# Attention units in another order on TensorE: matmuls grouped by tile shape, one reduction on GpSimd

## The chip, the cores and the metric

The kernel runs on one core of one Trainium2 chip. The metric is device time in microseconds (us) of one execution, the median of several runs. TensorE (PE) multiplies into PSUM; VectorE (DVE), ScalarE (ACT) and GpSimd (POOL) do the rest; SyncE (SP) issues the DMAs that this document speaks of.

## The reference

```python
def _attn_ref(q, k, v):                      # batch 4, heads 8, seq 576, head_dim 64
    q_d, k_d, v_d = means over groups of 4 positions          # 144 positions
    out_d = sm_attn(q_d, k_d, v_d)                            # full softmax, pooled
    out_up = np.repeat(out_d, 4, axis=2)
    mask = np.abs(pos[:, None] - pos[None, :]) < 4
    out_local = softmax(where(mask, q k^T / 8, -1e9)) v       # 7 keys per query
    return out_up + out_local

def reference(**kwargs):
    x = _attn_ref(q, k, v)        # as 2304 rows of 512
    x = _moe_ref(x, ...)          # soft MoE, 8 experts, 4 slots each: x @ phi, two softmaxes
    return _moe2_ref(x, ...)      # top-2 MoE, 8 experts, 512 -> 1024 -> 512
```

## The kernel before, in words

The program has three stages: the attention (about 0 to 160 us of the span), the soft MoE (to about 200), the top-2 MoE (the rest). The change touches the first alone.

The attention works on 16 **units**, each one batch and two heads. The loop over `p` from -1 to 14 walks the string `SEQ` of step names; the table `BL` gives each name its function and its offset: step f with offset d works on unit p - d. The end, units 13 to 15, is written out in `TSEQ`. Each engine gets its instructions in this order and works them off in order; nothing reorders them. All line numbers are those of the kernel before.

The steps, by engine:

- `ld` (L186, SP): queries and keys of unit p+2, four DMAs in pieces of 256 bytes, into one of two buffers. `lV` (L207, SP): values of unit p+1, four DMAs, into one of two buffers, whose readers `VD` and `DP` of unit p-1 stand in the same p. `W` (L101, SP): one half of a matrix of the soft MoE, 1 MB, in two or four DMAs. SP's order is ld, W, lV in each p.
- `A0`, `A1` (L231, PE): keys and queries of unit p+1 turned (12 passes); `a0x`, `a1xx`: copies out of PSUM into K and Q. `DQ0`, `DQ1` (L249 and L251 on POOL, L245 on DVE): sums of four neighbouring queries of each head; `KD` (L257, L258, POOL): the same of the keys.
- `S` (L285, L289, PE): the mask, then the scores of unit p, 40 passes of 35 columns in tiles of 128x64. `M`, `EL`, `EX`, `SU`, `P0`, `P1`: softmax on DVE, ACT, DVE and POOL (L333).
- `SD` (L300, PE): pooled scores; `MD`, `DX`, `RD`, `DM`: their softmax (L339 DVE, L351 ACT, L358 DVE, L365 POOL).
- `CP`, `CD` (L375, L386, PE): the two probability matrices of unit p-1 turned; `EPxx`, `EDx`: copies out.
- `VD` (L268, L272, PE): pooled values, in tiles of 128x32; `V0`, `V1`: copies out. `DP` (L414, PE): local product, tiles of 64x64; `x0`, `x1`: copies out. `DD` (L421, PE): pooled product, two heads by two blocks of 128 and 16 keys; `XA` (L433, DVE): adds it.
- `EP` (L441, L443, PE): the finished unit p-2 turned; `LG` (L463, L465, PE): its part of x @ phi, four matmuls with 32 columns of phi and one with phi four times side by side; `LA` (L474, DVE): adds it up.
- `ST`, `SU_`, `SK` (L506, L519, L534): once per batch, the softmax over rows and its product.

The helper `cp` puts a copy on DVE when its name is in `ON_V`, else on ACT. PSUM has four buffers `t`, one `S`, one `Sd`, one `xl` of two banks.

Of the kernel before, what the change touches and what calls it, by code (L numbers as in the profile page):

```python
# [25 lines left out]
ON_V = ['a110', 'a111', 'p00', 'v0', 'v1']  # L26
# [11 lines left out]
def attn_moe_moe_kernel(ctx: ExitStack, tc: tile.TileContext, q, k, v, moe_phi, moe_w1, moe_w2,  # L38
# [10 lines left out]
    NG = 10  # L49
# [40 lines left out]
    phi4 = const.tile([128, 4, 4 * NS], F32, name="phi4")  # L90
# [24 lines left out]
    with ExitStack() as tctx:  # L115
# [34 lines left out]
        P = a2.tile([128, NG, 64], F32, name="P")  # L150
        Vs = [(a1, a2)[i].tile([128, 5, 2, D], F32, name=f"V{i}") for i in range(2)]
# [27 lines left out]
        LD, VQ, KD, DQ, SD, SS, PD, PL, XL, XT, XK = ({} for _ in range(11))  # L179
# [81 lines left out]
        def v_pe(u):  # L261
# [21 lines left out]
        def b_s(u):  # L283
            s = ps.tile([128, 512], F32, name="S")
            nc.tensor.matmul(s[:, 0:NG * KW], idb, mask.rearrange("p g k -> p (g k)"), start=True, stop=True)  # L285
# [6 lines left out]
            SS[u] = s  # L292
# [87 lines left out]
        def c_d(u):  # L380
# [8 lines left out]
            PdT = wk.tile([128, 2, 2, 144], F32, name="PdT", bufs=1)  # L389
            CT[u, 1] = (PdT, tt)  # L390
# [8 lines left out]
        def c_ed(u, kb):  # L399
            PdT, tt = CT[u, 1]  # L400
# [36 lines left out]
        def e_pe(u):  # L437
# [148 lines left out]
        for p in range(-1, NU - 1):  # L586
# [8 lines left out]
            for nm in SEQ:  # L595
# [8 lines left out]
                if p == -1 and nm == "lV":  # L604
                    nc.gpsimd.memset(PT, 0.0)
# [797 lines left out]
```

## Time and profile before

| what | us |
|---|---|
| median of three runs (lowest, highest) | 496.54 (495.12, 497.39) |
| the profiled execution | 494.55 |
| its span, first to last instruction | 492.7 |
| attention: first score matmul (S of unit 0) to the soft MoE's first product (L795) | 8.42 to 164.37 |
| PE busy, share of the span | 470.2, 95% |
| DVE, ACT, POOL busy | 277.4, 263.4, 199.2 |

A time in a row is counted from the span's start. Matmuls overlap, so the time that a step takes on PE is read from its start to the start of the next step, not from its own duration.

### The profile page before, as it was taken

To read this page: it belongs to the slowest core of one execution; us is meant where nothing else is said; L and a number is where in the kernel's file an instruction comes from. 1 tells how busy PE (TensorE), PEld (TensorE's weight loads), DVE (VectorE), ACT (ScalarE), POOL (GpSimd) and SP (SyncE) were. 2 spreads that over 40 slices of the span, in tenths; PEclk is the share of its full clock that TensorE was granted. 3 is DMA by queue.
4 is the path that set the end of the run, shared out by engine and by line. 5 is a ranking of instruction groups with operands and counts; after the bars stand their busy time and mean duration, and the time that the engine had idled before them with its cause. 6 is when DMAs were issued, how large, how long until landed. Compare 5 with 4: busy or idle time off the path is not lost.

```text
span 492.7 us, 12033 instructions
## 1 busy us (share of the span) xinstructions
PE 470.2 (95%) x4569; PEld 355.9 (72%) x4569; DVE 277.4 (56%) x720; ACT 263.4 (53%) x698; POOL 199.2 (40%) x289
## 2 busy tenths in 40 slices
PE   5999999899998999899999999999999999999993
PEld 4688877777875543467787787887887887878882
DVE  7878877777875321696579545273462544624300
ACT  2567766666775021486365465483664746727410
POOL 5565636536540100166566677422222221222222
PEclk9999999999999799999999999999999999999997
DMA  9999998989979599999988744699958856333333
GB/s 160 278 243 214 233 221 192 242 216 202 265 239 345 171 393 399 389 346 338 365 258 228 224 75 76 150 363 297 275 72 229 216 128 154 43 45 43 45 43 46
DMA packets 108423, 104.16 MB, mean 211 GB/s; under 512 B 68170, under 2 KB 78090, under 8 KB 108362
## 3 DMA queue, kind: packets, MB, share of 16 engines
q1 hardware_dynamic: 101450, 90.50, 61.2%
q0 software_dynamic: 6912, 12.85, 16.6%
q8 instruction: 38, 0.62, 0.5%
q14 instruction: 23, 0.19, 0.1%
HBM read 83.60 MB, written 19.73 MB: 210 GB/s over the span
## 4 chain that ended last, share of the span: by engine, by line
PE 73%; issue 9%; DMA 7%; DVE 3%; POOL 2%; ACT 2%; POOLq 2%; SPq 0%; ACTq 0%; DVEq 0%
PE y L1054 34%; DMA wr<-in_moe_w_dram 5%; PE S L289 4%; PE t L231 3%; PE gx L871 3%; PE xl L421 3%; PE Sd L300 3%; PE xl L414 2%; PE t L375 2%; PE xl L268 2%; PE t L441 2%; PE h L1034 2%; PE t L386 2%; POOL out_dram L1073 2%; POOLq L1079 1%
## 5 line engine op out<-in xcount | busy, mean ns | idle before, releaser
L1054 PE MATMUL y<-whi,hl 128*128 128x512 f32 x320 | 127.3, 398 | 0.0
L1054 PE MATMUL y<-whi,hh 128*128 128x512 f32 x320 | 126.7, 396 | 0.4 <-ACT hh L1035 0.4
L1054 PE MATMUL y<-wlo,hh 128*128 128x512 f32 x320 | 126.5, 395 | 0.0
L1073 POOL DMA_INDIRECT out_dram<-ys,idx x40 | 64.5, 1612 | 107.9 <-ACT ys L1065 56.3
L1065 ACT ACTIVATE ys<-y,gt 128x512 f32<-128x512 f32 x40 | 27.4, 686 | 82.4 <-issue 46.9
L1026 DVE TENSOR_TENSOR wlo<-wr,whi 128x512 fp32r<-128x512 f32 x64 | 42.0, 692 | 50.3 <-ACT whi L1023 49.9
L1054 PEld LDWEIGHTS y<-wlo,hh 128*128 128x128 f32 x320 | 60.1, 188 | 12.9 <-issue 1.0
L1054 PEld LDWEIGHTS y<-whi,hl 128*128 128x128 f32 x320 | 60.1, 188 | 12.3 <-issue 2.1
L1054 PEld LDWEIGHTS y<-whi,hh 128*128 128x128 f32 x320 | 60.2, 188 | 11.8 <-ACT hh L1035 0.6
L333 POOL TENSOR_TENSOR P<-El,su 64x350 f32<-64x350 f32 x31 | 23.9, 772 | 59.7 <-DVE su L326 38.3
L1036 DVE SCALAR_TENSOR_TENSOR hl<-h,hh 128x256 fp32r<-128x256 f32 (+1 forms) x64 | 31.3, 489 | 16.0 <-ACT hh L1035 14.7
L1000 POOL DMA_INDIRECT tab<-stk,pos x36 | 35.6, 990 | 11.5 <-issue 10.7
L1036 DVE SCALAR_TENSOR_TENSOR hl<-gx,hh 128x256 fp32r<-128x256 f32 (+1 forms) x64 | 31.2, 487 | 10.7 <-ACT hh L1035 9.1
L1023 ACT ACTIVATE whi<-wr 128x512 fp32r<-128x512 f32 x64 | 36.9, 625 | 0.2
L1035 ACT ACTIVATE hh<-gx 128x256 fp32r<-128x256 f32 (+1 forms) x64 | 28.1, 439 | 15.0 <-PE gx L1034 12.5
L1035 ACT ACTIVATE hh<-h 128x256 fp32r<-128x256 f32 (+1 forms) x64 | 28.0, 437 | 12.5 <-PE h L1034 10.2
L1072 POOL MEMSET spacer<- 1x1 f32 x40 | 13.6, 340 | 41.6 <-issue 41.6
L219 ACT ACTIVATE PT<-t 64x256 f32<-64x256 f32 (+1 forms) x50 | 20.6, 417 | 13.5 <-PE t L375 12.7
L919 DVE TENSOR_TENSOR oh<-iot,R 128x256 fp32r<-128x256 f32 (+2 forms) x50 | 20.3, 439 | 11.4 <-PE xs L937 9.6
L231 PE MATMUL t<-idf,ld 96*128 96x96 f32 x192 | 21.1, 259 | 4.9 <-DMA ld<-in_k_dram 4.3
L219 ACT ACTIVATE xT<-xl 128x290 f32<-128x290 f32 x32 | 11.5, 411 | 26.2 <-PE xl L421 24.1
L289 PE MATMUL S<-K,Q 128*64 128x35 f32 x640 | 23.1, 231 | 2.2 <-issue 1.4
(301 smaller groups left out, 837.8 us busy)
## 6 DMA issues: line engine op xcount, KB each, us to landing
wr<-in_moe_w_dram SPq DMA_DIRECT2D x120, 256.0 KB, 5.6
wr<-in_moe_w_dram SPq DMA_DIRECT2D x56, 512.0 KB, 7.1
out_dram<-zero SPq DMA_DIRECT2D x20, 256.0 KB, 3.4
V<-in_v_dram SPq DMA_DIRECT2D x62, 80.0 KB, 5.2
ld<-in_k_dram SPq DMA_DIRECT2D x32, 144.0 KB, 4.7
ld<-in_q_dram SPq DMA_DIRECT2D x32, 144.0 KB, 4.4
XT<-tab SPq DMA_DIRECT2D x5, 320.0 KB, 5.6
tab<-zero SPq DMA_DIRECT2D x6, 256.0 KB, 4.8
```

The costliest lines, as they stand in the source:

```text
L219: nc.scalar.activation(dst, src, AF.Copy)
L231: nc.tensor.transpose(t[:, 96 * c:96 * c + 96], ld[:, i, 3 * j + c].rearrange("p h d -> p (h d)"), idf[0:96, 0:96])
L289: nc.tensor.matmul(s[64 * a:64 * a + 64, KW * g:KW * g + KW], Q[:, c0:c0 + 32].rearrange("p i h -> p (i h)"), K[:, c0:c0 + KW], start=Fals ...
L333: eng.tensor_tensor(P[as_, :, HQ * a:HQ * a + KW], El[as_], su[as_, :, None].to_broadcast([64, NG, KW]), op=ALU.mult)
L1000: st = nc.gpsimd.indirect_dma_start(out=tab, out_offset=bass.IndirectOffsetOnAxis(ap=pos[:, c, i:i + 1], axis=0), in_=stk[:, i].bitcast(F3 ...
L1023: nc.scalar.activation(whi[:, kk], wb(kk), AF.Copy)
L1026: eng.tensor_tensor(wlo[:, kk], wb(kk), whi[:, kk].bitcast(F32), op=ALU.subtract)
L1035: nc.scalar.activation(hh[:, f], h, AF.Relu)
L1036: nc.vector.scalar_tensor_tensor(hl[:, f], h, 0.0, hh[:, f].bitcast(F32), op0=ALU.max, op1=ALU.subtract)
L1054: nc.tensor.matmul(y, l[:, kk, ts_], r_[:, kk], start=(m == 0), stop=(m == 23))
L1065: nc.scalar.activation(ys, YS.pop((e, ti)), AF.Copy, scale=gt[:, ti:ti + 1])
L1073: st = nc.gpsimd.indirect_dma_start(out=out, out_offset=bass.IndirectOffsetOnAxis(ap=idx[:, ti:ti + 1], axis=0), in_=ys, in_offset=None, c ...
```

## The change

A new `SEQ` orders the steps of a unit anew; `ON_V` spreads the copies anew; `DD` and `XA` move from offset 1 to 2 (the pooled product of a unit is made after the next unit's scores); its second block of keys, 16 rows, is padded with zeros to 128 rows in fixed buffers `Vd` and `PdT`; the mask is put down in two halves of 64 columns; `LG` writes its product into the bank of `S` and its last matmul becomes four with 32 columns each; `DQ1` goes to POOL except for the last unit. `NW`, `NPRE` and the three functions that load are as before.

```diff
-SEQ = """S SK CP EP01 ld EP10 M EP00 ST SD CD z EP11 ED0 EL SS MD A0 ED1 EX a00 W a01 SU SU_ A1 P1 a100 a101
-a110 a111 P0 KD DQ0 VD z DP V0 V1 DQ1 DX EP LG DD x1 LA lV x0 X1 SE RD DM X0 XA""".split()
-TSEQ = """S:15 CP:14 W EP01:14 EP00:14 SD:15 M:15 EL:15 ...
+SEQ = """S ld DD A1 M a110 a100 A0 XA a111 a101 SD a00 a01 KD EL SK ST DQ0 CP SS EP01 EP11 EP10 EP00 MD VD SU_ LG V1 CD
+V0 LA EX ED1 DX W EP X1 SE X0 DQ1 ED0 SU P1 DP lV P0 x0 x1 RD DM""".split()
+TSEQ = """S:15 DD:13 XA:13 CP:14 W EP01:14 EP00:14 SD:15 M:15 EL:15 ...
-ON_V = ['a110', 'a111', 'p00', 'v0', 'v1']
+ON_V = ['p00', 'd0', 'd1', 'a100']
...
         def a_dve(u, h):
-            if h:
+            if h and u == NU - 1:
                 return nc.vector.tensor_reduce(out=Dq[hs, :, h], in_=Q[hs, 0:576, h].rearrange(
...
         def b_s(u):
-            nc.tensor.matmul(s[:, 0:NG * KW], idb, mask.rearrange("p g k -> p (g k)"), start=True, stop=True)
+            for a in range(2):
+                as_ = slice(64 * a, 64 * a + 64)
+                nc.tensor.matmul(s[as_, 0:NG * KW], idb[:, as_], mask.rearrange("p g k -> p (g k)"), start=True, stop=True,
+                                 skip_group_check=True)
...
-            SS[u] = s
+            SS[u] = SB[u] = s
...
         def d_d(u):
-            xl, PdT, Vd = XL[u], CT[u, 1][0], VQ.pop(u)[1]
-            for kb, n in enumerate((128, 16)):
+            xl = XL[u]
+            for kb in range(2):
                 for h in range(2):
-                    nc.tensor.matmul(xl[64 * h:64 * h + 64, 1, 290:434], Vd[0:n, kb, 64 * h:64 * h + 64], PdT[0:n, kb, h],
+                    nc.tensor.matmul(xl[64 * h:64 * h + 64, 1, 290:434], Vd[:, kb, 64 * h:64 * h + 64], PdT[:, kb, h],
...
-        def logit_pe(u, t2=None):
+        def logit_pe(u):
             xT, kk = XT[u], u % 4
-            L = (ET_[u][1] if t2 is None else t2)[:, 128:320]
+            L = SB[u + 2][:, 0:192] if not TAIL else ET_[u][1][:, 128:320] if u in ET_ else tp()[:, 0:192]
...
-            nc.tensor.matmul(L[:, 128:192], phi4[:, kk], xT[:, 512:576], start=True, stop=True, skip_group_check=True)
+            for t in range(4):
+                nc.tensor.matmul(L[32 * t:32 * t + 32, 128:192], phi[:, kk], xT[:, 512:576], start=True, stop=True,
+                                 skip_group_check=True)
...
-              "DD": (d_d, 1, ()), "XA": (d_add, 1, ()), ...
+              "DD": (d_d, 2, ()), "XA": (d_add, 2, ()), ...
```

PE, one unit in the middle of the attention, from the last logit matmul of a unit on (t, S, Sd, xl are PSUM tiles, ld the loaded queries and keys), before:

```order
L465 MATMUL t<-xT,phi_79 128x64
L421 MATMUL xl<-PdT,Vd 64x144 x4
L285 LDWEIGHTS idb
L285 MATMUL S<-mask,idb 128x350
L289 MATMUL S<-K,Q 64x35 x20
L375 MATMUL t<-idf,P 128x128 x5
L300 MATMUL Sd<-kd,Dq 96x144 x3
L386 MATMUL t<-idf,Ed 128x96 x3
L386 MATMUL t<-idf,Ed 16x96 x3
L231 MATMUL t<-idf,ld 128x96 x12
```

and with the change, from the scores on:

```order
L293 MATMUL S<-K,Q 64x35 x20
L424 MATMUL xl<-PdT,Vd 64x144 x4
L233 MATMUL t<-idf,ld 128x96 x12
L304 MATMUL Sd<-kd,Dq 96x144 x3
L379 MATMUL t<-idf,P 128x128 x5
L270 MATMUL xl<-V_135,four 32x128 x8
L274 MATMUL xl<-V_135,four 32x64 x2
L466 MATMUL S<-xT,phi 32x128 x4
L469 MATMUL S<-xT,phi 32x64 x4
L390 MATMUL t<-idf,Ed 128x96 x3
L390 MATMUL t<-idf,Ed 16x96 x3
```

The turn of the loaded queries and keys (L231, now L233) moved ahead of the pooled scores and of both probability turns; the pooled product moved behind the scores; the turn of the finished unit (L444, L446) and the local product (L417) end the unit.

POOL, one unit (s holds half sums), before:

```order
L257 TENSOR_TENSOR s_761<-K 128x288
L258 TENSOR_TENSOR kd<-s_761 128x144
L249 TENSOR_TENSOR s_764<-Q 64x288
L251 TENSOR_TENSOR Dq<-s_764 64x3x48
L365 TENSOR_TENSOR Ed<-Ed,rd 96x432
L333 TENSOR_TENSOR P<-El,su 64x10x35 x2
```

and with the change:

```order
L259 TENSOR_TENSOR s_1087<-K 128x288
L260 TENSOR_TENSOR kd<-s_1087 128x144
L251 TENSOR_TENSOR s_1092<-Q 64x288
L253 TENSOR_TENSOR Dq<-s_1092 64x3x48
L251 TENSOR_TENSOR s_1167<-Q 64x288
L253 TENSOR_TENSOR Dq<-s_1167 64x3x48
L337 TENSOR_TENSOR P<-El,su 64x10x35 x2
L369 TENSOR_TENSOR Ed<-Ed,rd 96x432
```

The second head's sums stand on POOL ahead of the products P. SP's list of DMAs is the same, row for row.

## Rows read from the trace of the kernel before

**Rows 1.** The page, part 2: busy share of the DMA engines in 40 slices.

```profile
DMA  9999998989979599999988744699958856333333
```

**Rows 2.** Windows: PE, PEld, DVE, ACT, POOL busy us, clock, DMA share, GB/s.

```profile
40.00:60.00 20.00, 20.00 (x368) 16.02 (x362) 16.09 (x41) 13.56 (x48) 12.62 (x20) 1.00 1.00 218
...
180.00:200.00 20.00, 19.70 (x245) 7.79 (x237) 3.10 (x10) 4.49 (x9) 2.42 (x5) 1.00 1.04 398
...
155.00:159.00 4.00, 3.11 (x29) 1.68 (x25) 2.79 (x14) 2.24 (x9) 0.00 (x0) 1.00 0.91 327
...
161.00:165.00 4.00, 4.00 (x23) 2.79 (x25) 1.26 (x4) 0.00 (x0) 2.04 (x21) 0.50 0.27 108
```

**Rows 3.** Timeline of PE, the unit with p = 5.

```profile
49.75 0.32 PE L285 MATMUL S<-mask,idb 128*128 128x350 bf16 x1
50.01 1.36 PE L289 MATMUL S<-K,Q 128*64 128x35 f32 x40
51.30 0.77 PE L375 MATMUL t<-idf,P 128*128 128x128 f32 x5
...
53.29 1.21 PE L231 MATMUL t<-idf,ld 96*128 96x96 f32 x12
...
56.64 0.42 PE L463 MATMUL t<-xT,phi 128*32 128x128 f32 x8
56.99 0.43 PE L465 MATMUL t<-xT,phi 128*128 128x64 f32 x2
57.36 0.86 PE L421 MATMUL xl<-PdT,Vd 128*64 128x144 f32 x8
58.15 0.32 PE L285 MATMUL S<-mask,idb 128*128 128x350 bf16 x1
```

**Rows 4.** Timeline of PE's weight loads, same unit.

```profile
57.75 0.19 PEld L421 LDWEIGHTS xl<-PdT,Vd 16*64 16x64 f32 x4 [0.20 <-issue]
```

**Rows 5.** Groups by line, 0 to 200 us: busy us, mean ns.

```profile
L249 POOL TENSOR_TENSOR s<-Q 64x288 f32<-64x288 f32 x16 | 15.1, 945 | 1.8 <-DVE Q L221 0.7
...
L221 DVE COPY Q<-t 64x288 f32<-64x288 f32 x34 | 14.3, 458 | 1.4 <-ACT Q L219 0.5 <-PE t L231 0.5
...
L245 DVE TENSOR_REDUCE Dq<-Q 64x144 f32<-64x576 f32 x16 | 12.0, 750 | 0.6
...
L251 POOL TENSOR_TENSOR Dq<-s 64x144 f32<-64x144 f32 x16 | 6.7, 419 | 1.3
```

**Rows 6.** Timeline of SP's queue, p = 4 to 5 and p = 13.

```profile
50.10 2.66 SPq L207 DMA_DIRECT2D V<-in_v_dram  x4
...
53.46 3.02 SPq L186 DMA_DIRECT2D ld<-in_k_dram  x2
56.52 1.14 SPq L186 DMA_DIRECT2D ld<-in_q_dram  x2
57.70 2.49 SPq L101 DMA_DIRECT2D wr<-in_moe_w_dram  x4
60.30 2.65 SPq L207 DMA_DIRECT2D V<-in_v_dram  x4
...
127.85 2.02 SPq L186 DMA_DIRECT2D ld<-in_q_dram  x2
...
131.93 3.44 SPq L207 DMA_DIRECT2D V<-in_v_dram  x4
```

**Rows 7.** DMA view: 40 to 130 us; then queries issued in 126.3 to 130, us to landing.

```profile
DMA packets 44144, 19.90 MB, mean 221 GB/s; under 512 B 40542, under 2 KB 40542, under 8 KB 44126
...
ld<-in_q_dram SPq DMA_DIRECT2D x2, 144.0 KB, 4.9
```

**Rows 8.** Timeline of PE: keys of unit 15 turned, scores of unit 15.

```profile
134.97 0.66 PE L231 MATMUL t<-idf,ld 96*128 96x96 f32 x6
...
141.53 1.36 PE L289 MATMUL S<-K,Q 128*64 128x35 f32 x40
```

**Rows 9.** Waits of SP's queue, 0 to 200 us: total, times, longest.

```profile
SPq L101 <- PE hp L795: 10.9, 5, 9.5
```

More of the change, by code (lines that the diff above doesn't have):

```diff
@@ L88, in attn_moe_moe_kernel @@
     fills = [t[r:min(r + 128, t.shape[0])] for t in (tabz, out) for r in range(0, t.shape[0], 128)]
-    phi4 = const.tile([128, 4, 4 * NS], F32, name="phi4")
+    phi = const.tile([128, 4, NS], F32, name="phi")
     wgn = const.tile([128, 4, 2 * E], F32, name="wgn")
@@ L150, in attn_moe_moe_kernel @@
         P = a2.tile([128, NG, 64], F32, name="P")
+        PdT = a2.tile([128, 2, 2, 144], F32, name="PdT")
+        Vd = a2.tile([128, 2, 128], F32, name="Vd")
         Vs = [(a1, a2)[i].tile([128, 5, 2, D], F32, name=f"V{i}") for i in range(2)]
@@ L177, in tp @@
             return ps.tile([128, 512], F32, name="t", bufs=4)
-        LD, VQ, KD, DQ, SD, SS, PD, PL, XL, XT, XK = ({} for _ in range(11))
+        LD, KD, DQ, SD, SS, SB, PD, PL, XL, XT, XK = ({} for _ in range(11))
         def load(u):
@@ L273, in v_pe @@
                                  skip_group_check=True)
-            VQ[u] = (None, wk.tile([128, 2, 128], F32, name="Vd", bufs=1))
         def v_evac(u, i):
-            xl, Vd = XL[u], VQ[u][1]
+            xl = XL[u]
             if i:
@@ L388, in c_d @@
                 tt.append(t)
-            PdT = wk.tile([128, 2, 2, 144], F32, name="PdT", bufs=1)
-            CT[u, 1] = (PdT, tt)
+            CT[u, 1] = tt
         def c_ep(u, i, g2):
@@ L399, in c_ed @@
         def c_ed(u, kb):
-            PdT, tt = CT[u, 1]
+            tt = CT[u, 1]
             n = (128, 16)[kb]
@@ L444, in e_pe, with e_evac @@
             ET_[u] = (t, t2)
-            if u % 4 == 0:
+        def e_evac(u, i):
+            if u // 4 not in XK:
                 XK[u // 4] = xp.tile([128, 5, 4, 128], F32, name="xK", bufs=1)
-        def e_evac(u, i):
             t = ET_[u][i]
@@ L457, in attn_moe_moe_kernel @@
         LL = {}
-        def logit_pe(u, t2=None):
+        def logit_pe(u):
             xT, kk = XT[u], u % 4
-            L = (ET_[u][1] if t2 is None else t2)[:, 128:320]
+            L = SB[u + 2][:, 0:192] if not TAIL else ET_[u][1][:, 128:320] if u in ET_ else tp()[:, 0:192]
             for t in range(4):
-                nc.tensor.matmul(L[32 * t:32 * t + 32, 0:128], phi4[:, kk, 0:NS], xT[:, 128 * t:128 * t + 128],
+                nc.tensor.matmul(L[32 * t:32 * t + 32, 0:128], phi[:, kk], xT[:, 128 * t:128 * t + 128],
                                  start=True, stop=True, skip_group_check=True)
-            nc.tensor.matmul(L[:, 128:192], phi4[:, kk], xT[:, 512:576], start=True, stop=True, skip_group_check=True)
+            for t in range(4):
+                nc.tensor.matmul(L[32 * t:32 * t + 32, 128:192], phi[:, kk], xT[:, 512:576], start=True, stop=True,
+                                 skip_group_check=True)
             LL[u] = L
@@ L558, in attn_moe_moe_kernel @@
               "DQ0": (a_dve, -1, (0,)), "DQ1": (a_dve, -1, (1,)), "KD": (a_pool, -1, ()), "DP": (d_pe, 1, ()),
-              "DD": (d_d, 1, ()), "XA": (d_add, 1, ()), "VD": (v_pe, 1, ()), "V0": (v_evac, 1, (0,)), "V1": (v_evac, 1, (1,)),
+              "DD": (d_d, 2, ()), "XA": (d_add, 2, ()), "VD": (v_pe, 1, ()), "V0": (v_evac, 1, (0,)), "V1": (v_evac, 1, (1,)),
               "ST": (slot_t, None, 1), "SU_": (slot_u, None, 1), "SS": (slot_sum, None, 1), "SK": (slot_k, None, 2),
@@ L587, in attn_moe_moe_kernel @@
             if p == 0:
-                nc.sync.dma_start(out=phi4[:, :, 0:NS], in_=moe_phi.rearrange("(k p) s -> p k s", p=128))
+                nc.sync.dma_start(out=phi, in_=moe_phi.rearrange("(k p) s -> p k s", p=128))
             if p >= 5 and small:
@@ L605, in attn_moe_moe_kernel @@
                     nc.gpsimd.memset(PT, 0.0)
+                    nc.gpsimd.memset(Vd[:, 1], 0.0)
+                    nc.gpsimd.memset(PdT[:, 1], 0.0)
                 if p == -1 and nm == "DQ1":
@@ L670, in attn_moe_moe_kernel @@
               "SI": slot_in, "UA": lambda: slot_u(B - 1, (0, 1)), "UB": lambda: slot_u(B - 1, (2, 3)),
-              "LG:15": lambda: logit_pe(NU - 1, tp()), "W": flush}
+              "W": flush}
         TAIL.append(1)
```

6 lines of the change are left out of this document (2 added, 4 removed).

## The prediction

> **What bounds the kernel now.** The page comes first: the 40 slices of the DMA engines stand at 8 or 9 tenths in the first eleven slices, to 135 us [rows 1]. Then the windows: from 40 to 60 us PE is busy all 20 us at full clock (1.00, its 2.4 GHz level), and DVE, ACT and POOL have 16.1, 13.6 and 12.6 of 20 [rows 2]. Then PE's timeline of one ordinary unit: mask to mask, 49.75 to 58.15, is 8.40 us [rows 3], and nothing in it waits for more than about 0.2 us. So PE sets the pace, by its own work. A unit's share on the others is 16.09 x 8.40/20 = 6.8 us on DVE, 5.7 on ACT, 5.3 on POOL.
>
> The view that I weigh most is SP's queue. It has no pause: values at 50.10, keys and queries at 53.46 and 56.52, a weight half at 57.70, values again at 60.30, and each piece ends where the next begins, but for small loads and about 0.1 us [rows 6]. The values at 60.30 overwrite a buffer whose last reader, the local product of p = 5, is on PE two steps ahead of the logit matmuls at 56.64 [rows 3]: SP comes some 4 us late for it and doesn't wait for PE. The loads of queries and keys wait for earlier DMAs only. So the transfers run at a pace of their own: from 50.10 to 131.93 are nine p, 81.83/9 = **9.09 us each** [rows 6]. PE's mean, with the once-per-batch steps, is nearly the same: scores at 50.01 and at 141.53 are ten units apart, 9.15 each [rows 3, 8]. Two chains of equal length run beside each other: PE and the transfers. What shortens one meets the other.
>
> How near they are at the end: the second load of queries of unit 15 is issued about 1.5 us after 127.85 and lands 4.9 later, so at about 134.0 (133.4 to 134.3) [rows 6, 7]. Its keys were turned at 134.97 [rows 8], its queries after the once-per-batch product, some 2 us later.
>
> **What the change takes away on PE.** A change of tile shape costs PE a pause: the weights for 16 rows follow those for 128 rows after 0.20 us without a load [rows 4], a pattern that stands ahead of five loads of that unit, where loads of one shape follow at once. Within a shape the next matmul starts about 0.1 us after the last, so a switch costs 0.10 us (bounds 0.05 and 0.20). Before, a unit has ten: mask to scores, scores to L375, L231 to L268, L272 to L414, L414 to L441, L443 to L463, L463 to L465, L465 to L421, within L421, L421 to mask. After, five: pooled product to L233, L379 to L270, L469 to L390, L446 to L417, L417 to mask. That is 5 x 0.10 = 0.50.
> - Wide logit matmul: 56.99 to 57.36 is 0.37, two switches' worth of it 0.2. Four narrow ones side by side: the eight passes of 128 columns at 56.64 take 0.35 with a switch, so 0.125 per four, half of it for 64 columns, 2 x 0.06 = 0.12 [rows 3]. Saved beside the switches: 0.05 to 0.10.
> - Pooled product: 57.36 to 58.15 is 0.79, less two switches 0.59 [rows 3]; the padded block streams the same 144 columns, but its first weights now load behind the scores: 0.10 saved.
> - The mask in two halves: two matmuls side by side, no gain or loss beyond 0.05.
> - L231 at 53.29 had waited about 0.15 for a PSUM buffer; now it comes when the buffers are long free: 0.15.
> Sum: 0.85 per unit (bounds 0.5 and 1.15), **7.55 us** in place of 8.40.
>
> **Other engines.** DVE gives away L245, 0.75, and has four copies of a unit where it had five, 0.46: 6.8 - 1.2 = 5.6. ACT has one copy more: 5.7 + 0.4 = 6.1. POOL gets 0.945 + 0.419 = 1.36: 6.7 [rows 2, 5]. All stay under 7.55, so I cost these moves at nothing. The cover is thinnest on POOL: P now stands behind both sums, and its next reader L379 comes only after scores, pooled product, L233 and L304. If the cover goes, POOL's 6.7 plus waits is the pace, still under 9.09.
>
> **What is late next.** L233 now stands right behind the pooled product, some 1.8 us into the unit, in place of 3.5 (49.75 to 53.29) [rows 3], and it needs queries first, which SP loads second. All later work of PE queues behind it, and on DVE the copy a100, then XA and EL. SP's list is the same, so queries land every 9.09 us on average, while PE could come every 7.55 plus 0.75 (9.15 less 8.40, once-per-batch work): 8.3. PE gains for a few units, uses up the lead that its loads now have, and from then waits about 0.8 us per unit at L233. **The gain per unit is given back as a wait for ld.** On the move of DP to the unit's end: lV, queued behind ld and W on SP, waits for it. DP ends 5.3 us after L233 starts (7.55 less 1.8 and 0.4 of mask and switch); for p = 5, whose loads had landed when L231 ran at 53.29, that is at most 53.29 + 5.3 = 58.6, and SP comes to lV at 60.30, 1.7 later [rows 3, 6]. A once-per-batch unit is about 1.7 longer and has nothing to spare. So I cost it at nothing, with 0.5 per unit as the other bound.
>
> **The sum at the end.** L233 of unit 15 starts at 134.0. In the kernel before, 134.97 to 141.53 is 6.56 [rows 8]. Behind L233 come now also L304, L379, L390, 51.30 to 53.29 = 2.0 [rows 3], and 0.2 of L506; out of that stretch go the pooled product 0.79, the wide logit matmul 0.25, four switches 0.4, the wait 0.15. So 7.2, and the scores of unit 15 start at 141.2, 0.3 earlier. After it, the tail has the pooled product of unit 13 in addition (0.5), against three logit products shorter by 0.25 and two pooled ones shorter by 0.3: 1.35 - 0.5 = 0.85 saved. The tail hangs on chains through other engines too, so I count half of it, 0.4. Together **-0.7 us** (bounds -3 and +2). The soft MoE starts with L795, and the next weight loads wait for it (9.5 us the longest) [rows 9], so the rest moves with it, one to one.
>
> Against the profiled execution: 494.55 - 0.7 = 493.85. The median of the runs shown is 2.0 above the profiled one, so the forecast on that scale is 495.8. About 0.5% (2.5 us) is what a measurement of this kernel can tell from no change.
>
> **A rule against the row.** 90 us moved 19.90 MB in 44144 packets, 40542 of them under 512 bytes, at 221 GB/s [rows 7], with the engines' share at 1.00, while large packets made 398 GB/s at 1.04 [rows 2]; so small packets fill the engines at about half the bytes, and I take 9.09. The Trainium skill (DMA: Bandwidth & Descriptors, Specifications) gives about 358 GB/s as a core's limit from HBM; a unit's 2 MB would need about 5.6 us by it, an estimate, and the transfers would hold nobody. The same list says that transfers below 512 bytes miss line rate, and with that the trace agrees.
>
> **The rivals.**
> - *The transfers follow PE* (0.22, faster). For it: PE did not wait for ld in [rows 3], and two chains are seldom of one length by chance, so SP may follow PE in a way that the rows don't show. Against it: SP comes late for lV [rows 3, 6]. (The Trainium skill's 358 GB/s, above, speaks for this one.) Then 13 units gain 0.85 to 1.15, 11 to 15 us: about 484 on the median's scale, half of it (490) where only some waits vanish.
> - *The clock falls* (0.13, slower). PE would now idle about 0.8 us in each unit. From 155 to 159 it was busy 3.11 of 4 us at clock 1.00, and from 161 to 165 it ran at 0.50, the 1.2 GHz level [rows 2]. A 4 us stretch at half clock costs 2 us, more than the 0.8 that the unit has to spare; with one such stretch in half of 13 units, 6 x (2 - 0.8) = 7 us: 503. It decides from the first unit in which the wait is long enough to lose the clock. Against it: 3.11 of 4 is a lower share than 8.3 of 9.1.
> - *SP waits for DP* (0.10, slower). If DP ends more than 1.7 us later than worked out in an ordinary unit, or at all later in the once-per-batch ones, SP stands at lV, and the next ld with it: 0.3 to 0.5 us x 13 = 4 to 6 us: 501. Against it: the 1.7 [rows 3, 6].
> - *The switch isn't what costs* (0.03): the pauses stay and the wait shrinks; the end is the same.
>
> **The chances.** Forecast 0.52, of which 0.05 goes under -2.5 us. Faster by over 0.5%: 0.22 + 0.05 = 0.27; slower: 0.13 + 0.10 = 0.23; within: 0.50. The range takes the bounds, half of the first rival and most of the slower ones: 487 to 502.
>
> **What would show it.** Right: L233 waits for ld in most units, the unit's period stays near 9 us in the mean, loads of L421's second block follow without the 0.20, PE falls to about 18 of 20 us busy in the window from 40 to 60, SP's period stays 9.09. Wrong: SP standing idle at lV, periods near 7.6, the landing of unit 15's queries well before 133, a clock under 1.00 before 150 us, or scores waiting for EL, LA or P.

## The result, and the profile after

The change made the kernel slower: 497.94 us (median of 20 runs, 494.43 to 502.26) against 494.60 (20 runs beside them), ratio **1.0078, 95% interval 1.0053 to 1.0103**. The forecast was 495.8, no change. The profiled execution is the longest of its twenty, 502.26 (span 500.0, mean clock 0.972), so its trace shows more of the loss than the median has; four others, of 500.0 to 500.9 us, have a mean clock as low.

First the waits of PE from 16 us to 145 us, in the changed kernel: engine, line, what it waited for; total, times, longest. In the kernel before the same view has 2.4 us in all, none of it for loads.

```profile
PE t L233 <- DMA ld<-in_q_dram: 6.4, 6, 1.6
PE xl L424 <- ACT xT L221: 5.2, 7, 1.6
```

The first line is the forecast one: the turn of queries stands still for its load. The second, as long, was not forecast: the pooled product, now behind the next scores, waits for ScalarE to copy out the product that shares its tile. Over the whole run the group of L233 has 12.5 us of idle time for queries, half of it in the first 16 us. The expectations below speak of these 12.5; the text gives the runs from 16 us on, 6.4 here.

```profile
L233 PE MATMUL t<-idf,ld 96*128 96x96 f32 x192 | 23.6, 285 | 12.7 <-DMA ld<-in_q_dram 12.5
```

The transfers are what they were, 220 GB/s in 43860 packets against 221 in 44144 [rows 7]; DMA view, 40 to 130 us:

```profile
DMA packets 43860, 19.83 MB, mean 220 GB/s; under 512 B 40258, under 2 KB 40258, under 8 KB 43842
```

What the clock did is in the windows (columns as in [rows 2]). The page's line of the clock, in 40 slices of 12.5 us, is below 9 in the attention's slices 4, 9 and 12, and again in 14 (the soft MoE), 18 and the last:

```profile
PEclk9998999989989799979999999999999999999998
```

In the windows come first 40 to 60 us, which answers to [rows 2]; then pairs, 2 us ahead of a fall of the clock and the stretch behind them:

```profile
40.00:60.00 20.00, 18.05 (x368) 16.21 (x365) 12.51 (x34) 12.88 (x46) 13.65 (x21) 0.91 1.02 214
...
43.00:45.00 2.00, 0.71 (x8) 0.47 (x9) 0.46 (x1) 0.14 (x1) 1.93 (x3) 0.99 0.92 214
45.00:48.40 3.40, 3.39 (x19) 3.39 (x20) 1.54 (x3) 1.85 (x5) 0.69 (x2) 0.50 1.15 296
97.50:99.50 2.00, 0.41 (x12) 0.30 (x10) 1.48 (x7) 1.82 (x8) 0.81 (x2) 1.00 0.87 203
99.60:103.00 3.40, 3.40 (x23) 3.02 (x20) 1.30 (x3) 1.69 (x5) 1.50 (x2) 0.50 0.92 261
135.10:137.10 2.00, 1.03 (x13) 0.83 (x13) 0.64 (x4) 0.92 (x3) 1.72 (x3) 1.00 1.02 340
137.20:140.50 3.30, 3.30 (x19) 3.25 (x18) 2.36 (x5) 1.87 (x6) 1.62 (x3) 0.50 1.02 248
217.00:219.00 2.00, 2.00 (x12) 1.56 (x11) 2.00 (x7) 1.93 (x5) 0.50 (x1) 1.00 1.05 354
219.10:225.80 6.70, 6.23 (x18) 4.93 (x18) 5.66 (x11) 3.53 (x9) 6.06 (x9) 0.50 1.05 347
```

Three times PE is busy 0.41 to 1.03 of 2 us, and each time the granted clock then stands at 0.50, its 1.2 GHz level. The kernel before has no such record before 159 us. But four more stretches of the changed kernel look the same, and no fall follows them:

```profile
34.00:36.00 2.00, 0.73 (x9) 0.49 (x9) 0.48 (x1) 0.16 (x1) 1.93 (x3) 1.00 0.82 215
62.00:64.00 2.00, 0.71 (x8) 0.44 (x8) 0.23 (x1) 0.54 (x2) 1.92 (x3) 1.00 0.96 318
89.00:91.00 2.00, 0.41 (x8) 0.17 (x5) 0.00 (x0) 0.00 (x0) 1.51 (x2) 1.00 0.73 215
117.70:119.70 2.00, 0.90 (x21) 0.66 (x17) 0.52 (x1) 0.13 (x1) 1.93 (x3) 1.00 1.00 347
```

The kernel before has one, with 0.60 of 2 us busy from 93.7 on, and it too keeps its clock. So one such stretch does not settle whether the clock falls; three of the changed kernel's seven had a fall behind them. PE's timeline has the waits that went ahead of the falls, of L233 once and of L424 twice:

```profile
45.01 2.15 PE L233 MATMUL t<-idf,ld 96*128 96x96 f32 x12 [1.10 <-DMA ld<-in_q_dram]
...
99.38 1.08 PE L424 MATMUL xl<-PdT,Vd 128*64 128x144 f32 x8 [1.59 <-ACT xT L221]
...
136.07 0.71 PE L424 MATMUL xl<-PdT,Vd 128*64 128x144 f32 x8 [1.38 <-ACT xT L221]
```

L233's block takes 2.15 us there, against 1.18 in a unit at full clock and 1.21 before [rows 3]. ScalarE's timeline says why L424 waits, by 1.0 to 1.6 us in a unit with slots: the slots' exponentials and a copy of xK are done ahead of the two copies of xT.

```profile
133.93 0.40 ACT L491 ACTIVATE ET<-LT,nm 128x128 f32<-128x128 f32 x1 [0.27 <-DVE nm L488]
...
134.84 0.57 ACT L221 ACTIVATE xK<-t 128x512 f32<-128x512 f32 x1
135.32 0.70 ACT L221 ACTIVATE xT<-xl 128x290 f32<-128x290 f32 x2
```

In the profile the mask of unit 15 starts at 145.4 us (141.3 before), the soft MoE at 169.7 (164.4), the top-2 stage's first product with an expert's weights (L871, now L875) at 207.0 (201.9), and the last expert product 7.0 us later than before. The last 1.9 of these come with a fourth fall, at 219 us. PE was busy all 2 us ahead of it (217 to 219 us above), so no wait of the attention explains that one.

**Over all runs.** Each run has a span and a mean clock, so its time at the lower level is 2 x (1 - clock) x span. Within kernels, over 218 runs of this study, 1 us at the lower level goes with 0.35 us of span (standard error 0.02). The kernel before has 11.6 us at the lower level on average (80 runs, mean span 492.8), the changed one 21.1 (20 runs, 496.0): 9.5 x 0.35 = 3.3 us, the whole difference of 3.2. At full clock both come to the same, 488.8 and 488.7. The 0.35 could hide that runs with more waiting have a lower clock and a longer span for one reason; against that, the kernel before, whose attention hardly waits, has 0.40 by itself (standard error 0.03), the changed one 0.31 (0.05). And at one clock the two are equally long: runs with a mean clock of 0.980 to 0.987 have a span of 494.4 us before (32 runs) and of 494.1 with the change (9 runs).

### The profile page after: what moved, and what is told of

It is laid out like the page before. It is cut to its first block, busy times and chain, and to the rows that moved or that the text cites. A ratio compares the mean times of both kernels' runs of the same rounds, so it can differ in the third digit from the quotient of the medians.

```text
span 500.0 us, 12249 instructions
## 1 busy us (share of the span) xinstructions
PE 467.4 (93%) x4681; PEld 362.6 (73%) x4681; DVE 265.2 (53%) x689; ACT 265.8 (53%) x713; POOL 220.0 (44%) x321
## 4 chain that ended last, share of the span: by engine, by line
PE 47%; issue 4%; DVE 1%; POOLq 1%; ACT 1%; POOL 1%; DVEq 0%
PE y L1058 39%; PE gx L875 3%; PE h L1038 2%; PE gx L1038 2%; POOLq L1083 1%; DVE hl L1040 1%; PE xs L941 1%; POOL out_dram L1077 1%; PE xs L1019 1%; PE xs L938 0%; DVE wlo L1030 0%; ACT ys L1069 0%; PE gx L955 0%; ACT hh L1039 0%; ACT whi L1027 0%
## 5 line engine op out<-in xcount | busy, mean ns | idle before, releaser
L1058 PEld LDWEIGHTS y<-wlo,hh 128*128 128x128 f32 x320 | 60.7, 190 | 13.1 <-issue 1.0
L1004 POOL DMA_INDIRECT tab<-stk,pos x36 | 35.5, 986 | 11.5 <-issue 10.7
L1040 DVE SCALAR_TENSOR_TENSOR hl<-gx,hh 128x256 fp32r<-128x256 f32 (+1 forms) x64 | 31.3, 488 | 11.2 <-ACT hh L1039 8.8
L233 PE MATMUL t<-idf,ld 96*128 96x96 f32 x192 | 23.6, 285 | 12.7 <-DMA ld<-in_q_dram 12.5
L221 ACT ACTIVATE Q<-t 64x288 f32<-64x288 f32 x45 | 17.8, 424 | 30.5 <-PE t L233 26.1
L233 PEld LDWEIGHTS t<-idf,ld 96*128 96x128 f32 x192 | 20.4, 165 | 15.8 <-issue 15.7
L337 POOL TENSOR_TENSOR P<-El,su 64x350 f32<-64x350 f32 x31 | 24.0, 773 | 15.5 <-DVE rd L362 11.3
L251 POOL TENSOR_TENSOR s<-Q 64x288 f32<-64x288 f32 x31 | 29.6, 953 | 2.4
L923 DVE TENSOR_TENSOR oh<-iot,R 128x256 fp32r<-128x256 f32 (+2 forms) x50 | 20.6, 446 | 13.1 <-PE xs L941 11.2
```

The source lines that it names most:

```text
L233: nc.tensor.transpose(t[:, 96 * c:96 * c + 96], ld[:, i, 3 * j + c].rearrange("p h d -> p (h d)"), idf[0:96, 0:96])
L251: nc.gpsimd.tensor_tensor(q2, q4[:, :, 0:2], q4[:, :, 2:4], op=ALU.add)
L337: eng.tensor_tensor(P[as_, :, HQ * a:HQ * a + KW], El[as_], su[as_, :, None].to_broadcast([64, NG, KW]), op=ALU.mult)
L923: OH_I.append((nc.vector if eng == "v" else nc.gpsimd).tensor_tensor(oh[:, 0:w], iot[:, lo:hi], R[:, i, e:e + 1].to_broadcast([128, w]), o ...
L1004: st = nc.gpsimd.indirect_dma_start(out=tab, out_offset=bass.IndirectOffsetOnAxis(ap=pos[:, c, i:i + 1], axis=0), in_=stk[:, i].bitcast(F3 ...
L1040: nc.vector.scalar_tensor_tensor(hl[:, f], h, 0.0, hh[:, f].bitcast(F32), op0=ALU.max, op1=ALU.subtract)
```

## The experiments

"Scores" is the start of the mask of unit 15 in the profiled run, "low" the mean time at the lower clock over a kernel's runs, "at full clock" the mean span less 0.35 x low. Ratios are to the kernel before on the same chip, with 95% intervals; in brackets behind "low" stands the mean of the runs of the kernel before beside it (for the change they have no record of the clock).

| run | ratio | scores | low | at full clock |
|---|---|---|---|---|
| before | 1 | 141.3 | 11.6 | 488.8 |
| the change | 1.0078 (1.0053 to 1.0103) | 145.4 | 21.1 | 488.7 |
| e3 fill 4 | 1.0083 (1.0051 to 1.0115) | 144.7 | 9.5 (9.6) | 492.7 |
| e4 sums on VectorE | 1.0051 (1.0019 to 1.0084) | 146.7 | 18.0 (9.6) | 488.8 |
| e5 loads ahead | 1.0195 (1.0115 to 1.0276) | 152.0 | 24.1 (11.1) | 492.9 |
| e6 four weights later | 1.0129 (1.0045 to 1.0212) | 140.2 | 25.4 (11.1) | 488.6 |
| e7 both, and slots | 1.0130 (1.0050 to 1.0211) | 141.4 | 24.9 (11.1) | 489.2 |
| e8 before, two sizes | 0.9942 (0.9902 to 0.9982) | 140.2 | 11.7 (11.1) | 484.9 |
| e9 turns later | 1.0308 (1.0263 to 1.0354) | 161.3 | 15.5 (14.0) | 504.1 |
| e10 before, three sizes | **0.9926 (0.9896 to 0.9957)** | 140.3 | 11.2 (14.0) | 485.5 |
| e11 before, loads behind weights | 1.0248 (1.0185 to 1.0311) | 156.5 | 23.5 (14.0) | 499.3 |
| e12 turns later, slots | 1.0329 (1.0285 to 1.0373) | 156.7 | 15.1 (14.0) | 504.4 |
| e13 e10 + GpSimd's sums | 1.0223 (1.0163 to 1.0282) | 155.7 | 20.8 (13.1) | 497.6 |
| e14 e10 + pooled moved | 0.9941 (0.9905 to 0.9977) | 139.3 | 13.7 (13.1) | 485.6 |
| e15 e14 + turns | 1.0226 (1.0162 to 1.0290) | 155.4 | 15.0 (13.1) | 499.2 |
| e16 old spread | 1.0222 (1.0162 to 1.0282) | 153.3 | 10.6 (13.1) | 500.5 |
| e17 old sizes | 1.0126 (1.0088 to 1.0164) | 143.8 | 17.2 (10.2) | 490.5 |
| e18 fill 2 | 1.0081 (1.0051 to 1.0111) | 147.7 | 12.9 (10.2) | 490.5 |

### What PE needs by itself: e1 and e2

Both kernels without the expert weights among the attention's transfers:

```diff
-NW = [2] + [1] * 14
+NW = [0] * 15
```

> The changed kernel with no expert weights sent between the units of the attention (all sixteen halves are issued behind the last unit, so the whole kernel's time says nothing; only the attention is read). Theory A (in the changed kernel the transfers set the unit, TensorE waits for the queries there, and its clock falls behind such waits): without the weights the units come to 7.5 to 7.7 us, the wait of the turns for the queries falls from 12.5 us to under 2 us, the last scores start before 133 us (145.4 us in the changed kernel's profile), and no record of the lower clock lies between 40 us and the last scores. Rival B (the reordered chain over ScalarE, VectorE or GpSimd sets the unit): the units stay at 8.2 us or more with the weights gone, and the last scores start after 139 us.

> The kernel before, with the same weights left out of the attention. Theory A: TensorE bounds the unit there, so units stay at 8.39 us (units with the slots' work 10.0 and less as before) and the last scores start at 138 to 141.5 us (141.3 before). The difference to the run of the changed kernel without weights is then what the change is worth on TensorE: 0.7 to 0.9 us a unit. Rival (transfers bound the kernel before as well): the units shorten below 8.2 us and the last scores start before 137 us.

Scores at 136.0 and 139.9 us. The changed kernel's units without slots come mostly every 7.76 to 7.88 us, those of the kernel before every 8.39 as with the weights. Windows of 40 to 90 us (columns as above), the changed kernel without weights and then the kernel before without them: PE is busy 48.08 and 50.00 of 50 us, with the transfers at half load.

```profile
40.00:90.00 50.00, 48.08 (x1006) 41.85 (x1005) 36.94 (x100) 37.30 (x133) 37.83 (x56) 1.00 0.56 115
```

```profile
40.00:90.00 50.00, 50.00 (x874) 39.89 (x873) 39.17 (x103) 34.30 (x117) 27.83 (x41) 1.00 0.53 109
```

In 50 us the first gets through 1006 matmuls, the second through 874, though some of the difference is the blocks that are now two or four. So on PE the change is worth about 0.55 us in a unit without slots, less than the 0.7 to 0.9 of e2's expectation, and nothing in the units with slots (10.2, 12.4 and 10.7 us against 10.0, 10.2 and 10.2, with a fall of the clock in the second). By the scores of unit 15 that is 3.9 us in all. With the weights there the changed kernel loses 145.4 - 136.0 = 9.4 us, the kernel before 1.4. The waits of the first, 16 to 145 us:

```profile
PE xl L424 <- ACT xT L221: 5.4, 7, 1.6
...
PE t L233 <- DMA ld<-in_q_dram: 1.1, 2, 0.8
```

The wait for queries goes from 6.4 to 1.1 us: it hangs on the transfers. The wait for ScalarE stays, and so did one fall of 3.4 us at 93.5, behind such a wait, against the expectation of none. Units and scores are also a little longer and later than Theory A's 7.5 to 7.7 and 133.

### Is it the wait or the clock: e3 and e18

Filling on PE, n = 4 or 2, where it would wait:

```diff
-            sd = ps.tile([128, 512], F32, name="Sd")
+            sd = SD.pop(u) if u in SD else ps.tile([128, 512], F32, name="Sd")
...
+        def fill(u):
+            if 2 <= u < NU - 1:
+                SD[u] = ps.tile([128, 512], F32, name="Sd")
+                hot(n, SD[u])
-SEQ = """S ld DD A1 ...
+SEQ = """S ld DD FL A1 ...
```

> The changed kernel with four more 512-column multiplications of ones on TensorE (about 0.85 us) between the pooled product and the queries' turn in units 2 to 14, into the bank of the next pooled scores; their result is thrown away. Theory A (the loss is the clock that falls behind the wait): TensorE is busy where it waited, no lower clock is recorded between 40 us and the last scores (three falls of 3.4 us in the changed kernel's profile), the last scores start at 141 to 142.5 us, and the time is 493.5 to 496 us, 0.996 to 1.003 of the kernel before. Rival C (the wait itself is the loss, the clock only goes with it): the time stays at 497.5 to 499 us, and if the filling is not covered by the wait it goes up to 505 us.

> The changed kernel with two filling multiplications in a unit (0.43 us) instead of the four tried (which held the clock, 9.5 us at the lower level on average, but cost 3.8 us of span at full clock). Theory A: 9 to 15 us at the lower level on average instead of 21, the filling mostly hidden in the waits, 492.5 to 496 us. Rival C (clock and wait are not linked, or the filling is not covered): 497 us or more.

Four kept the clock: no fall before 214 us, and low drops from 21.1 to 9.5, as in the kernel before beside it (9.6). But 13 fillings of 0.86 us add 11 us, and ordinary units are now 8.71 us, 0.86 more than the 7.85 of e1; at full clock the span is 4.0 longer, and the time the same as with the change. Two give 12.9 and 1.8: the same again. So idle PE time has a part in the fall of the clock, shown by putting work into it; but the fillings buy the clock at its price, and no run shows what the kernel gains when the clock holds at no cost. Neither reached the time that Theory A named; by its time alone e3 lies where Rival C put it, and what speaks against Rival C is the comparison at one clock above. e3 still waits 5.7 us for ScalarE, with stretches as idle as those ahead of the falls, and the clock holds:

```profile
97.50:99.50 2.00, 0.54 (x8) 0.44 (x8) 1.06 (x6) 1.41 (x6) 1.23 (x2) 1.00 0.94 305
134.30:136.30 2.00, 0.42 (x14) 0.31 (x12) 1.52 (x7) 1.87 (x8) 0.81 (x2) 1.00 1.05 346
```

Which of the two waits does it, the table can narrow down. In the kernels whose profile has over 3 us of waits for loads from 16 to 145 us (e4 to e7, e11, e17, e18), low is 3 to 14 us above the kernel before beside it. In the others it is within 3 us of it, though PE waits up to 19 us there for other engines (e9, e16). e13 is the exception: 12.0 us of waits for GpSimd, up to 1.9 at a time, and 8 us more. This is a comparison between kernels; e1 had a fall behind a wait for ScalarE alone.

### Bringing the loads sooner: e5, e6, e7

```diff
-SEQ = """S ld DD ... DP lV P0 ...
+SEQ = """S DD ... DP ld lV P0 ...
-"ld": (load, -2, ())
+"ld": (load, -3, ())
+load(1)
```

> The changed kernel with the loads of queries and keys a unit earlier in SyncE's order: they are issued right ahead of the values' loads, for the unit after the one that they were for, so that they no longer stand behind four loads of values and a wait for the pooled and local product. No byte is added or taken away. Theory A1 (the turn waits because of the order of the transfers; the values have some 5 us to spare): the turns' wait for the queries falls from 12.5 us to under 2 us, at most one lower clock before the last scores, which start at 136 to 140 us; time 490 to 495 us, 0.992 to 1.002 of before. Rival A2 (the rate of the transfers is the bound, whatever their order): the wait moves to the keys, the values or the buffers, the last scores start after 143 us, and the time stays at 497 to 499 us.

A miss in both theories' numbers, and worse than the change: scores at 152.0. The wait for queries is 8.0 us. SyncE now stands still ahead of the values' loads: the waits that the view puts down to PE there are 24.4 us against 10.8 in the changed kernel, half of the 10.8 in pieces of 0.5. The transfers move 208 GB/s from 40 to 130 us in place of 220. The largest group (SP's waits, 16 to 145 us):

```profile
SPq L209 <- PE t L446: 11.4, 7, 2.7
```

This order of the loads is no cure; with it the transfers themselves are slower.

```diff
-NW = [2] + [1] * 14
+NW = [1, 1, 1, 0, 1] * 3
```

> The changed kernel with one half of an expert's weights sent in four of five units instead of every one (none in units 3, 8 and 13, one in the first where there were two); the four that are left follow the last unit, where the transfers had 0.70 of their engines' time in the changed kernel. Theory A2 (rate): the wait for the queries falls to 3 to 7 us of 12.5, the last scores start at 139 to 142 us, and the time is 493 to 496.5 us if the four are hidden behind the end of the attention. Theory A1 (order): the wait stays at 9 us or more, and the time at 497 to 499 us. Rival: the four are late for the first experts, the stage after the attention begins no earlier (207 us in the changed kernel) and the time stays or rises.

Waits for queries 3.3 us (9.5 over the whole run, where the rate's theory said 3 to 7 of 12.5), scores 5.2 us earlier than with the change, as that theory says. Low is no smaller, 25.4. Most of the 5.2 is given back behind: from the soft MoE's first product to the top-2 stage's (L875) it takes 41.0 us (164.2 to 205.2) in place of 37.3, and there PE waits for weights:

```profile
PE hp L799 <- DMA wr<-in_moe_w_dram: 2.1, 4, 0.7
```

The windows of 160 to 200 us, of e6 and then of the changed kernel:

```profile
160.00:200.00 40.00, 37.76 (x411) 15.49 (x407) 8.45 (x28) 5.71 (x11) 3.61 (x26) 0.92 1.04 396
```

```profile
160.00:200.00 40.00, 39.24 (x450) 17.98 (x452) 12.28 (x47) 7.88 (x20) 3.62 (x26) 0.91 0.89 330
```

With the DMA engines at 1.04 there (0.89 with the change), the bytes moved out of the attention find little room behind it, and over the runs the kernel is no faster than the change.

e7 has both edits and the slots' `SE` moved behind `x0 x1`:

> Both of the two edits before, and the slots' exponentials behind the evacuations of the product instead of ahead of them on ScalarE (the pooled product waited 5.2 us for those evacuations in the units with slots). If wait and clock are the whole loss: last scores at 133 to 137 us, no lower clock ahead of them, time 486 to 492 us. If the stage after the attention is bound by the weights' transfers all the same: last scores as early, but the first product of the top-2 stage at 200 us or later, and 492 to 495 us.

The wait for ScalarE falls to 2.0 us, no time is gained: scores at 141.4, L871's product (now L876) at 206.0. Neither case holds: the scores are not as early as 133 to 137, and the time is worse than in both.

### Part by part from the other end: e8, e10, e14, e13, e15

The kernel before in its own order, with the mask in two halves and the logits' last product in four (e8); with the padded pooled product too (e10).

```diff
-            nc.tensor.matmul(s[:, 0:NG * KW], idb, mask...
+            for a in range(2):
+                nc.tensor.matmul(s[as_, 0:NG * KW], idb[:, as_], mask...
-            nc.tensor.matmul(L[:, 128:192], phi4[:, kk], xT[:, 512:576], ...
+            for t in range(4):
+                nc.tensor.matmul(L[32 * t:32 * t + 32, 128:192], phi4[:, kk, 0:NS], xT[:, 512:576], ...
```

> The kernel before, in its own order, with two of the changed block sizes alone: the mask written by two products of 64 columns of weights, the logits of the last columns by four of 32. Theory: two changes of the tile's shape fewer on TensorE, units of 8.1 to 8.3 us (8.39 before), and nothing else moves; the last scores start at 139.5 to 141.5 us and the time is 493 to 495 us (0.997 to 1.001). Rival (the sizes themselves cost TensorE time): units of 8.4 us or more.

> The kernel before with the two block sizes of the run before and the third: the pooled product with all 128 rows (values and probabilities in buffers zeroed once). Theory: the tail of 16 rows cost a change of the tile's shape, units of 7.85 to 8.0 us, time 489.5 to 492 us (0.990 to 0.997). Rival: TensorE reaches the loads, as in the changed kernel: waits for the queries over 3 us and 493 us or more.

Both are faster than either kernel: 490.68 and 490.72 us, at full clock 3.0 and 3.7 us less than the kernel before beside them, low nearly unchanged. Units of e8 are 8.00 us, 0.39 less. PE's timeline of e8:

```profile
47.57 0.43 PE L466 MATMUL t<-xT,phi 128*32 128x128 f32 x8
47.81 0.29 PE L469 MATMUL t<-xT,phi 128*32 128x64 f32 x8
48.04 0.86 PE L424 MATMUL xl<-PdT,Vd 128*64 128x144 f32 x8
48.82 0.34 PE L287 MATMUL S<-mask,idb 128*64 128x350 bf16 x2
```

Two switches are gone, between mask and scores and between the narrow and the wide logit product. The logits, start of L466 to start of L424, take 0.47 in place of 0.72 [rows 3]; the mask and the scores, to the start of the turn behind them, 1.41 in place of 1.55. By the prediction's terms that is 2 x 0.10 and 0.05 to 0.10 for the wide product, 0.25 to 0.30. The Trainium skill (TensorEngine Tiling (Array Packing), Key Properties) says that a change of tiling mode drains TensorE; the 0.39 us agrees. The third size shows at its place, but not in the unit. In e10 the pooled product, start to start, takes 0.54 in place of 0.78, and the pooled scores (L304) then start 0.83 behind the turn L379 in place of 0.60, because they wait for GpSimd's sums; the unit stays at 8.00:

```profile
39.87 0.71 PE L424 MATMUL xl<-PdT,Vd 128*64 128x144 f32 x8
40.41 0.32 PE L288 MATMUL S<-mask,idb 128*64 128x350 bf16 x2
...
41.80 0.77 PE L379 MATMUL t<-idf,P 128*128 128x128 f32 x5
42.63 0.98 PE L304 MATMUL Sd<-kd,Dq 128*96 128x144 f32 x6
```

PE waits for queries 1.3 us in e10, less than in pauses that the view puts down to nothing ("issue"):

```profile
PE S L293 <- issue: 3.8, 3, 1.8
PE t L233 <- DMA ld<-in_q_dram: 1.3, 2, 0.7
```

The three pauses stand in the middle of the scores' block, and none is followed by a fall, though one leaves PE busy for 0.24 of 2 us; the kernel before has one of 1.4 us. With them e10's fourteen units from the mask at 14.8 to that at 140.3 are 8.96 us in the mean, against 9.06 before: in this profile PE does not run far ahead of its loads, so e10 does not show what a quicker PE meets there. Most of its gain in the profiled run lies behind unit 15. From here towards the change: the pooled product moved (`S DD ...`, offsets 2), sums on GpSimd alone, and pooled product and turns moved.

> The kernel before with the three sizes, and the pooled product behind the next unit's scores as in the change; the turns stay in their old place, which comes 0.7 us later in the unit. Theory A: the turns do not wait for the loads, 488.5 to 491.5 us (0.986 to 0.995). Rival E (the moved product delays the outputs' sums and the logits behind them): 492 us or more.

> The kernel before with the three new block sizes (0.993 of before) and the queries' second sums on GpSimd as in the change; order and copies as before. Theory A (the place of the turns is the loss): the same as the sizes alone within 1 us, 490 to 492 us (0.990 to 0.997), lower clock 9 to 13 us on average. Rival D (GpSimd's work, late sums): 1.5 us or more over the sizes alone, with waits of the pooled scores for GpSimd's sums of over 3 us.

> The same with the turns of the coming unit right behind the pooled product, and their evacuations ahead of the probabilities', as in the change. Theory A: this is the piece that loses: waits for the queries of 6 us or more, lower clock 16 to 25 us on average, 495 to 500 us (1.000 to 1.010), that is 4 us or more over the run without the turns' move. Rival (the turns' place is harmless): within 1.5 us of the run without it.

The pooled product's move is harmless: 0.9941, 485.6 at full clock. The other two cost 12 and 14 us at full clock, but not by the mechanism under test: the pooled scores wait for GpSimd's sums. In e13:

```profile
PE Sd L304 <- POOL Dq L253: 12.0, 10, 1.9
```

In e15 the same wait is 10.9 us, and PE never comes early enough to wait for queries. Rival D holds in the old order; in the new order, where the sums have more room, undoing the move gains little or nothing (e4).

### Inside the changed kernel: e4, e16, e17, e9, e12

One part undone each: `if h:` in `a_dve` (e4); the old `ON_V` (e16); the three old sizes (e17).

> The changed kernel with the second half's sums of the queries back on VectorE. Theory A: off the path, 497 to 499 us (1.005 to 1.010 of the kernel before), the wait for the queries stays at 10 us or more. Rival D (GpSimd's extra work, or what it does to VectorE beside it, is the loss): back to 494 to 495.5 us.

> The changed kernel with the table of the copies on VectorE as before. Theory A: order of the turns is the loss and the copies are beside it, 496.5 to 499.5 us (1.003 to 1.011). Rival F (the new spread puts ScalarE or VectorE behind TensorE): 495 us or less.

> The changed kernel with the three old block sizes (mask by one product of 128 columns, the logits' last columns by one of 128, the pooled product's tail with 16 rows): order, GpSimd's sums and copies as changed. Theory A (TensorE runs ahead of its loads and its clock falls in the waits): TensorE's own unit is longer by 0.3 to 0.5 us, the waits for the queries fall to 3 to 8 us, lower clock for 10 to 17 us on average, and the time is 493 to 497.5 us, no slower than with the new sizes although TensorE has more to do. Rival G (the order costs by itself, the sizes gain in it as they do in the old order): 499 us or more, 1.010 of before or more.

e4: 496.74 us, between the two theories' numbers; its interval overlaps the change's. e16: 505.86 us, a miss for both: with the old table ScalarE and VectorE hold PE up, by 8.0 us at L379, 6.2 at L424 and 4.8 at L417. The new spread belongs to the new order. e17: 498.01 us; the wait for queries is 3.6 us and low 17.2, between before and the change. Its time lies between the two theories' numbers, its ratio where Rival G put it, above the change's with intervals that overlap. So the sizes may gain in the new order what they gain in the old one; these runs cannot tell.

Turns later in the unit (e9), and `SE` later too (e12):

```diff
-S ld DD A1 M a110 a100 A0 XA a111 a101 SD a00 a01 KD EL SK ST DQ0 CP SS EP01 EP11 EP10 EP00 MD
+S ld DD M XA SD EL SK ST CP A1 EP01 EP11 a110 a100 A0 EP10 EP00 a111 a101 a00 a01 KD DQ0 SS MD
```

> The changed kernel with the turns of queries and keys, their evacuations and the keys' sums moved behind the pooled scores and the turn of the probabilities, as they stood before: some 1.5 us later in the unit; block sizes, GpSimd's sums and the spread of copies stay. Theory A (the turns' new place next to the pooled product puts them ahead of their loads; TensorE waits and its clock falls): the wait for the queries falls from 12.5 us to under 4 us, the time at the lower clock from 21 us on average over the runs to 8 to 14 us (before: 10), and the time from 498 us to 490 to 494.5 us, 0.990 to 1.002 of before. Rival (rate: with a shorter unit the transfers are late wherever the turns stand): the wait stays over 8 us and the time at 496 us or more.

> The changed kernel with the turns later (as above) and the slots' exponentials behind the product's evacuations on ScalarE. If the pooled product's wait for those evacuations (5.2 us in eight units) matters: 1 to 3 us less than with the turns later alone, 488 to 493 us. If it is covered by the transfers: the same within 1 us.

Both fail: 511 us. From 16 us on the wait for queries is gone, but the turns now wait for PSUM buffers that the probabilities' copies free:

```profile
PE t L233 <- ACT PT L221: 11.9, 13, 1.0
```

Units are 9.5 us, so the runs don't say what the turns' place costs in a quick unit.

### The control: e11

```diff
-EP01 ld EP10 ... a00 W a01
+EP01 EP10 ... a00 W ld a01
```

> The kernel before with one move in SyncE's order: the loads of queries and keys behind the unit's weights instead of ahead of them, which brings them 2 to 3 us later, where they had 1 to 3 us to spare; TensorE's own work and order stay. Theory A (a wait for the queries of under 1 us a unit is enough to lower the clock, and that is the loss): waits of the turns for the loads of 6 us or more, lower clock for 15 to 25 us instead of 10, and 496 to 500 us (1.004 to 1.012), as with the change, though no block, copy or sum of the change is in it. Rival C (a wait that the transfers would have cost anyway is free): under 495 us, with the waits in the trace.

The kernel before with its loads late: waits of L231 for loads of 5.2 us, low 23.5 against 14.0 beside it, and 510.17 us, 1.0248 where 1.012 was the most expected. At full clock it is 10.2 us longer than before, and the clock costs 3.3 on top. It is no clean control, though: PE's waits from 16 to 145 us come to 11.7 us in all, and SyncE's queue, ahead of the values' loads, stands 33.8 us against 15.4 by its view, and the transfers move 200 GB/s from 40 to 130 us where they moved 221. So more than the loads of queries and keys came late. Theory A's sign held, its size did not.

## Why the prediction was wrong

1. **"PE sets the pace": right.** PE without weights keeps 8.39 (e2). **"The transfers run at a pace of their own", 9.09 each: too strong.** The 220 GB/s after the change are the 221 of before, but e8 moved the same loads at 227 and e14 at 225, with fourteen units in (139.3 - 15.0)/14 = 8.88. So 9.09 is no floor; the transfers' rate alone did not hold the change at 220.
2. **The gain on PE, 0.85 per unit: right in kind, too large.** Without weights it is 0.55 in a unit without slots (bounds 0.5 and 1.15) and nothing in one with slots. In the old order the sizes are worth what the terms say or more: 0.39 in e8 against 0.25 to 0.30, and 0.24 for the padded block in e10 against 0.20 for the switches within it and behind it.
3. **"The gain per unit is given back as a wait for ld": right in part.** 6.4 us over the units from 16 us on is 0.5 each where 0.8 was forecast, and e1, with 1.1, shows that the wait hangs on the transfers.
4. **The step that failed** is the sum at the end, "the scores of unit 15 start at 141.2 ... Together -0.7 us": it let PE stand still 0.8 us per unit, charged that time with the gain alone and put the clock behind it at nothing. At full clock the forecast of no change holds, 488.7 against 488.8. The rival "The clock falls" had the mechanism, at a chance of 0.13; the forecast's own idle time is part of its cause. Measured: 9.5 us more at the lower clock, 3.3 us. In the profile, 141.2 and three falls of 3.4 us at 0.35 are 144.8; the trace has 145.4. That they meet is in part luck, as the gain was too large and the wait of point 5 missing. The rival's 503 was too dear: it took half of 13 units with a loss of 1.2 each, the trace has three falls. "3.11 of 4 is a lower share than 8.3 of 9.1" spoke against it by a mean over the unit; the idle time comes in pieces, and seven of them left PE busy 0.41 to 1.03 of 2 us, three with a fall behind.
5. **A wait that no step had**: the pooled product for ScalarE's copies of xT, 5.2 us. "ACT has one copy more: 5.7 + 0.4 = 6.1 ... I cost these moves at nothing" looked at ScalarE's sum, not at what stands ahead of those copies in a unit with slots. Two of the three falls came behind it. Taking it away (e7) gained nothing that shows, so its part in the loss stays open.
6. **"SP waits for DP"**: hardly. The waits of SP's queue for L417 were 3.1 us from 16 to 140 us (1.5 for L414 before), under the 4 to 6 that this rival took.
7. **Faster, "the transfers follow PE"**: no for the change; that they can go faster with another kernel is in point 1.

Left open: the fall at 219 us behind a busy PE; why three of seven like stretches lose the clock; what the pauses in the scores' block are; and how the loss divides over order, sums and spread, which only work together (e13, e15, e16). In the change the turns stand about 1.6 us earlier behind the mask than in e10 (1.98 against 3.63), and it turns the queries first, which SyncE loads second, where the kernel before turns the keys first. All of the change's waits for loads are for queries. No run turned the keys first, or loaded the queries first, in the new order.

## What to carry to other kernels

When a forecast makes TensorE wait, charge the wait twice: for its time and, with a chance, for the clock behind it, at a price taken from runs. Where transfers and TensorE run side by side at one pace, take first the parts of a change that shorten TensorE without moving its reads towards their loads: here the block sizes alone, in the old order, gave 0.993, and the same sizes with a new order 1.008. Look for a saving at its place in the timeline before calling it absent: the padded block's was there, and a wait behind it took it. Parts that were fitted to each other can't be priced one at a time: undoing the copies' table alone took the ratio from 1.008 to 1.022.

## What the runs showed of the hardware

- In the attention of the changed kernel the granted clock fell to its 1.2 GHz level three times, each time behind 2 us with TensorE busy 0.41 to 1.03. Four more such stretches there (0.41 to 0.90) and others in the kernel before (0.60), e3 (0.54 and 0.42) and e10 (0.24) were not followed by a fall, and the fall at 219 us came behind 2 us of a busy engine.
- 1 us at the lower level went with 0.35 us of span over 218 runs of these kernels (0.40 in the kernel before alone).
- Two changes of tile shape fewer in a unit, with one wide product in four narrow ones, were 0.39 us (8.39 to 8.00).
- The same loads moved at 200 GB/s (e11), 208 (e5), 221 (before) and 227 (e8) from 40 to 130 us; their order and TensorE's pace differed.
